# A gated mix of attention and a gated unit: a fixed table of seven PSUM banks, weights laid out by tiles, loads in order of use, maxima 20 steps ahead

## The chip, the cores and the metric

The kernel runs on one core of a Trainium2 chip. The metric is device time in microseconds (us); the kernel before takes 1745.21 us, the median of 3 runs (1744.91 to 1745.61). Smaller is better.

## What is computed

```python
def reference(x, wqkv, wo, w_gate, w_up, w_down, gate_w):     # x: 2048 x 512
    g = sigmoid((x * gate_w).sum(-1, keepdims=True))
    q, k, v = heads(x @ wqkv)                    # 32 heads of 16
    p = softmax(q @ k.T * 16 ** -0.5)            # per head, 2048 x 2048
    a = concat(p @ v) @ wo
    b = (sigmoid(x @ w_gate) * (x @ w_up)) @ w_down      # inner width 1792
    return g * a + (1 - g) * b
```

Everything is float32. Products of the projections are made of three products of a high and a low half each (`terms`, L126), so that the fast matmul form keeps the accuracy.

## The kernel before

The order of every engine's work is written out by hand: the program emits instructions in one stream, each engine keeps the order of emission, and waits come from the tiles that instructions share. PE is TensorE, ACT ScalarE, DVE VectorE, POOL GpSimd; SP only issues DMAs, in order.

**PSUM.** There are eight banks of 128 x 512: `st0..st2` (`banks`, L61), `dn` (L63), `sm0..sm3` (`maxb`, L65). `turns` (L54) hands out the banks of a list in rotation. A product may go into a bank only when the last reader of what stood there is done.

**Start (L222 to L346).** Twenty matmuls on zeros come first (`WARM`, L78). Then x is loaded in four chunks of 512 tokens (`load_x`, L179, one DMA for each 128 rows) and split into halves on ACT (high) and DVE (low) (`split_x`, L186). For each chunk, the first q tile and the first k tile are projected (12 matmuls each, L339 to L342) and put out to DRAM through ACT and DVE (`put_first`, L197); `load_pair` (L214) reads them back in the layout of a pair of heads, `QS` and `KS`. In chunk 3 the weights of v are split (L335 to L338). A weight tile is a block of 128 columns, loaded as 512 B rows (`raw_cols`, L105).

**Projection of v (L379 to L405).** Two token tiles at a time, each product cut into the lower and the upper 64 rows of the array (`Sum`, L135), so that two matmuls run side by side: one uses rows 0 to 63, the other rows 64 to 127. Between them run the first maxima: `first_max` (L322) makes steps 0 to 19 (`FIRST`) of the score maxima. At the end, `ahead` makes the first four score tiles. `turn` (L155) puts an empty instruction on POOL between two halves of a sum that write one bank: it waits for the first half, and the second half waits for it.

**The main loop (L534 to L565): 256 periods.** Softmax needs the maximum of each row of scores before the exponentials. So each period k has
- 4 + 4 score products of the pass for maxima, `m0` and `m1` (L254): rows 0 to 47 and 64 to 111 of the array for the two heads of a pair; DVE reduces each bank to one column (L256);
- 4 + 4 score tiles `t0` (this period's, lower rows) and `t1` (next period's, upper rows), L374; ACT takes the exponential of each (L376) into `p`;
- 6 + 6 half products of the side work `d1` (upper rows) and `d0` (lower rows), L146, into `dn`: projections of the other q and k tiles and of gate and up. Every second period a sum is finished, ACT copies it out (`leave`, L316), SP stores it;
- `values(k)` (L474): 8 products of v with p, in four column groups of the array at once (L482; the trace shows 16 instructions). They go into the next bank of the `st` list and are copied out by ACT (`part`, L487) and summed on POOL (L499).

The order of a period is the string `STEADY` (L526); the last 8 periods use `LAST`. The maxima run ahead of the exponentials: by 20 steps (a period is two steps) at first and, since one more product in each of the periods 0 to 3 (L546) moves them on, by 21 (`LEAD`) from there. When all 16 steps of half a pair are done, DVE reduces and transposes the maxima (L260, L262), POOL splits them, SP writes them to DRAM and reads them back into four rows of `QS` (`put_max`, L265); the score tiles of that half can only be made then.

The banks in the loop: `t0`, `t1` and `values` take `st0..st2` in rotation, nine uses a period; `m0`, `m1` take `sm0..sm3`. From the period in which the maxima are done, all seven are one list (`bank7`, L408).

**Behind the loop** follow the rest of the side work, the down projection and the output projection (L569 to L679), which the change leaves alone.

Of the kernel before, what the change touches and what calls it, by code (L numbers as in the profile page):

```python
# [34 lines left out]
FIRST = 20  # L35
LEAD = 21
WARM = 20
# [7 lines left out]
def gated_mix(ctx, tc, x, xT, wqkv, wo, w_gate, w_up, w_down, gate_w, out):  # L45
# [59 lines left out]
    def raw_cols(src, c0, name):  # L105
        return raw_weights(src[:, c0:c0 + P].rearrange("(k p) f -> p k f", p=P), [P, KT, P], name)
# [72 lines left out]
    def load_x(c):  # L179
        raw = mid(f"x{c}")  # L180
        cols = slice(c * 512, (c + 1) * 512)
        for k in range(KT):
            sp.dma_start(raw[:, k, :], xT[k * P:(k + 1) * P, cols])
        return raw

    def split_x(c, raw):  # L186
        cols = slice(c * 512, (c + 1) * 512)
        for k in range(KT):
            split(xh[:, k, cols], xl[:, k, cols], raw[:, k, :], act, dve)
# [35 lines left out]
    w_q = split_weights(raw_cols(wqkv, 0, "q0"), act, dve)  # L225
    xr = {0: load_x(0)}
# [3 lines left out]
    split_x(0, xr.pop(0))  # L230
    w_k = split_weights(raw_cols(wqkv, D, "k0"), act, dve)
# [33 lines left out]
    def put_max(half):  # L265
# [5 lines left out]
        def low():  # L271
# [3 lines left out]
            for b in range(2):  # L275
# [10 lines left out]
    def filling():  # L286
        jobs = [("qk", c) for c in range(1, D // P)] + [("gu", f) for f in range(NF)] + [("down", 0)]

        def raws(kind, n):
            if kind == "qk":  # L290
                return [raw_cols(wqkv, n * P, f"q{n}"), raw_cols(wqkv, D + n * P, f"k{n}")]
            if kind == "gu":
                return [raw_cols(w_gate, n * P, f"g{n}"), raw_cols(w_up, n * P, f"u{n}")]
# [25 lines left out]

    first = [(j, i) for j in [*range(0, 16, 2), *range(1, 16, 2), *range(16, FIRST)] for i in range(2)]  # L320

# [7 lines left out]
    for c in range(NC):  # L329
        if c + 1 < NC:  # L330
            split_x(c + 1, xr.pop(c + 1))
        if c == 0:
            wv_r = mid("wv_r")
            sp.dma_start(wv_r, wqkv[:, 2 * D:].rearrange("(k p) f -> p k f", p=P))
        if c == NC - 1:  # L335
# [3 lines left out]
        for w, dst in ((w_q, q_d), (w_k, k_d)):  # L339
            o = bank()  # L340
            product(o, unit(w, c))
            put_first(o, dst, c)  # L342
# [5 lines left out]
    bankv = turns(banks + [bankd()])  # L348
# [30 lines left out]
    bank = turns(banks[:2])  # L379
# [5 lines left out]
    for t in range(2, NS, 2):  # L385
        two = [Sum(bankv(), tokens(t + a)) for a in range(2)]
        for g in (LOW, UP):
            first_max()
            for m in range(3 * KT):
# [4 lines left out]
                if (0, 0) in mrow:  # L394
                    for step in put_max((0, 0)):
                        step()
                if t == NS - 2 and g == UP and m % 3 == 1:
# [10 lines left out]
    bank7 = turns(maxb + banks)  # L408
# [65 lines left out]
    def values(k):  # L474
# [10 lines left out]
        def put(e):  # L485
            if 2 * k + LEAD <= NSTEP:
# [16 lines left out]
    def mx(b):  # L503
        for j in range(FIRST, NSTEP):
# [11 lines left out]

    def emit(order, **parts):

        for kind in order.split():
            if kind == "turn":  # L520
                turn(run)
                work(1)
            else:
                next(parts[kind], None)

    STEADY = ("t0 m1 m0 d1 t0 d1 m0 d1 t0 d1 m0 d1 t0 d1 turn m0 t1 "  # L526
# [172 lines left out]
```

## Time and profile before

| | |
|---|---|
| median of 3 runs | 1745.21 us |
| the profiled execution | 1748.52 us, of which the span from the first to the last instruction is 1745.4 us |
| granted TensorE clock | 1.000 |
| busy: PE, DVE, ACT, POOL | 1737.6, 1426.0, 1318.7, 469.7 us |
| the main loop (products L482 of period 4 to those of period 244) | 118.58 to 1468.79 us |

A timeline row has the start in us from the span's start, the duration, the engine (PEld is the loading of weights on PE; SPq a DMA issue), line, operation, what is written and read, and how many instructions were merged; in brackets stands the idle time of the engine just before and what ended it. A row of the stretches has the stretch, its length, then busy time and instructions of each engine, the granted clock, the DMA share and GB/s. In the chain of waits each piece has start, duration, engine, tile and line.

### The profile page before, as it was taken

The numbers are of one execution on the slowest core, as the hardware profiler recorded it, in microseconds if no ns is written. First come the engines' busy times: TensorE is split into PE (matmuls) and PEld (weight loads), VectorE is DVE, ScalarE is ACT, GpSimd is POOL, SyncE is SP. The second block draws the span as 40 slices with busy tenths as digits, with TensorE's granted clock in tenths as the row PEclk, the third lists the DMA queues.
The fourth block names the chain that finished last, engine by engine and source line by source line (L and its number), as shares of the span: only waits on it lengthen the run. The fifth ranks groups of instructions, "written<-read, shape, count | busy, mean of one in ns | idle before, by whom it ended". The sixth has DMA issues, their size and how long they took to land.

```text
span 1745.4 us, 33221 instructions
## 1 busy us (share of the span) xinstructions
PE 1737.6 (100%) x12676; PEld 1041.8 (60%) x12676; DVE 1426.0 (82%) x2292; ACT 1318.7 (76%) x2554; POOL 469.7 (27%) x437
## 2 busy tenths in 40 slices
PE   9999999999999999999999999999999999999999
PEld 7755555555555555555555555555555555588887
DVE  5988888888988899989888888888888886357543
ACT  4188888888888888888888888888888888853321
POOL 1024343422231222222222222222222222352110
PEclk9999999999999999999999999999999999999999
DMA  8312424241313131414131313122121312367752
GB/s 248 80 32 68 92 68 92 68 105 44 81 52 76 41 87 51 86 51 87 38 75 39 68 39 62 51 55 53 50 51 49 63 45 80 105 228 247 258 193 73
DMA packets 99167, 149.74 MB, mean 86 GB/s; under 512 B 18816, under 2 KB 45440, under 8 KB 96128
## 3 DMA queue, kind: packets, MB, share of 16 engines
q1 hardware_dynamic: 99008, 147.63, 31.0%
q8 instruction: 99, 1.62, 0.4%
q14 instruction: 60, 0.49, 0.1%
HBM read 87.56 MB, written 60.03 MB: 85 GB/s over the span
## 4 chain that ended last, share of the span: by engine, by line
PE 96%; DVE 3%; DMA 1%; ACT 0%; issue 0%; POOL 0%; DVEq 0%; ACTq 0%; POOLq 0%
PE st L482 26%; PE st L374 20%; PE dn L146 18%; PE sm L254 16%; PE sm L662 7%; PE st L133 3%; DVE stat L256 2%; PE dn L662 2%; PE sm L571 1%; PE sm L482 1%; DMA k_d<-qe 1%; PE st L571 1%; PE st L146 1%; PE sm L374 0%; PE st L79 0%
## 5 line engine op out<-in xcount | busy, mean ns | idle before, releaser
L256 DVE TENSOR_REDUCE stat<-sm 128x1 f32<-128x512 f32 x2048 | 1250.1, 682 | 164.2 <-PE sm L254 138.3
L376 ACT ACTIVATE p<-st 128x512 f32<-128x512 f32 x2005 | 1012.4, 641 | 6.5 <-PE st L374 6.2
L374 PE MATMUL st<-qs,ks 64*128 64x512 f32 x2005 | 823.4, 423 | 0.0
L254 PE MATMUL sm<-ks,qs 48*128 48x512 f32 x2048 | 798.4, 417 | 0.4
L374 PEld LDWEIGHTS st<-qs,ks 64*128 64x128 f32 x2005 | 367.4, 184 | 327.5 <-ACT p L376 104.3
L499 POOL TENSOR_TENSOR sum<-sum,part 128x512 f32<-128x512 f32 x224 | 289.4, 1292 | 885.7 <-PE sm L254 674.9
L482 PE MATMUL st<-p,v 128*17 128x512 f32 x3984 | 476.1, 595 | 0.0
L254 PEld LDWEIGHTS sm<-ks,qs 48*128 48x128 f32 x2048 | 356.8, 185 | 61.1 <-DVE stat L256 16.4
L487 ACT ACTIVATE part<-st 128x512 f32<-128x512 f32 x215 | 128.6, 598 | 180.9 <-PE st L482 176.8
L482 PEld LDWEIGHTS st<-p,v 128*17 128x17 f32 x3984 | 92.3, 96 | 232.3 <-issue 156.0
L447 DVE TENSOR_TENSOR gul<-gul 128x1024 f32<-128x1024 f32 (+1 forms) x30 | 46.8, 1565 | 34.8 <-ACT gul L446 32.2
L316 ACT ACTIVATE gu<-dn 128x512 f32<-128x512 f32 x99 | 69.2, 699 | 0.0
L662 PE MATMUL sm<-wd_h,hl 128*128 128x512 f32 x208 | 67.0, 389 | 0.0
L95 ACT ACTIVATE hl<-gul 128x1024 fp32r<-128x1024 f32 (+1 forms) x30 | 29.8, 996 | 33.8 <-PE sm L662 22.0
L95 ACT ACTIVATE oh<-ot 128x1024 fp32r<-128x1024 f32 x8 | 8.5, 1062 | 59.9 <-DVE ot L620 59.9
L98 POOL TENSOR_TENSOR ol<-ot,oh 128x1024 fp32r<-128x1024 f32 x8 | 19.3, 2409 | 110.0 <-ACT oh L95 110.0
L98 DVE TENSOR_TENSOR hl<-gul,hl 128x1024 fp32r<-128x1024 f32 (+1 forms) x30 | 42.3, 1417 | 4.1 <-ACT hl L95 4.0
L662 PEld LDWEIGHTS sm<-wd_h,hl 128*128 128x128 f32 x208 | 39.0, 188 | 8.2
L487 ACT ACTIVATE sum<-st 128x512 f32<-128x512 f32 x31 | 18.5, 598 | 32.8 <-PE st L482 32.8
L662 PE MATMUL sm<-wd_l,hl 128*128 128x512 f32 x104 | 40.5, 389 | 0.0
L357 ACT ACTIVATE v<-st 128x512 f32<-128x512 f32 x12 | 6.9, 597 | 44.4 <-PE sm L254 25.2
L133 PE MATMUL st<-wohl,oh 128*128 128x512 f32 x128 | 39.4, 389 | 0.0
(454 smaller groups left out, 2821.4 us busy)
## 6 DMA issues: line engine op xcount, KB each, us to landing
gu_d<-gu SPq DMA_DIRECT2D x112, 256.0 KB
gul<-gu_d SPq DMA_DIRECT2D x56, 512.0 KB
qs<-q_d SPq DMA_DIRECT2D x90, 128.0 KB
ks<-k_d SPq DMA_DIRECT2D x90, 128.0 KB
pv_d<-sum SPq DMA_DIRECT2D x32, 256.0 KB
q_d<-qe SPq DMA_DIRECT2D x12, 512.0 KB
k_d<-qe SPq DMA_DIRECT2D x12, 512.0 KB
x<-in_xT_dram SPq DMA_DIRECT2D x16, 256.0 KB
```

Of the source, the lines that this page charges most:

```text
L98: lo.tensor_tensor(l, src, h.bitcast(F32), ALU.subtract)
L133: pe.matmul(o, a, b, start=(i == 0), stop=(i == len(ops) - 1))
L146: mm = pe.matmul(self.o, a[rows], b[rows], start=(self.n == 0), stop=(self.n == 2 * len(self.ops) - 1))
L254: pe.matmul(t, qs[r:r + KM, qt * P:(qt + 1) * P], ks[r:r + KM, g * 512:(g + 1) * 512], start=True, stop=True)
L256: dve.tensor_reduce(stat[half][:, b, qt % 8, g:g + 1], t, axis=AX.X, op=ALU.max)
L316: leave = lambda e, o: act.activation(e, o, AF.Copy)
L374: pe.matmul(o, ks[r:r + KR, (kt + a) * P:(kt + a + 1) * P], qs[r:r + KR, q0:q0 + 512], start=True, stop=True)
L376: act.activation(pt[:, 2 * a + c, :], o, AF.Exp, scale=DH ** -0.5)
L482: pe.matmul(o[32 * c:32 * c + VW, :], v[:, 2 * k % 16 + a, h * VW:(h + 1) * VW], pts[c // 2][:, 2 * a + c % 2, :], start=(a == 0), stop=(a ...
L487: act.activation(e, o, AF.Copy)
L499: pool.tensor_tensor(s, s, e, ALU.add)
L662: pe.matmul(down[t], a, b, start=(f == 0 and m == 0), stop=(f == NF - 2 and m == 5))
```

## The change

- **Banks.** In the loop each `t`, `m` names its bank in the order string, an index into `seven = sm0..sm3, st0..st2`: 0 to 3 are `sm`, 4 to 6 `st`. `values` always takes bank 0 (`SUMS`). The order of a period differs too: `m1` comes first, and in the first half the pieces of one row half come in twos (`d1 d1`).
- **Maxima.** `LEAD` is 20; `FIRST` and the extra maxima of periods 0 to 3 go. The maximum of half a pair is then complete at the end of a period, not three quarters through it. Its rows for the upper head are read back first.
- **Loads.** The host lays q, k, gate and up weights out by tiles, so that a partition's part of a tile is one run of 2 KB. At the start the order is q tile, x rows 0 and 1, k tile, x rows 2 and 3, and chunk 0 is projected in two parts: q and k with the first two row blocks, then q and k with the others. `WARM` is 10. The weights of v are split in chunk 2.
- **Last value tiles.** The v projection begins its rotation with `dn`, so that the last pair of tiles is in `st1` and `st2`, both copied out by ACT; `ahead` uses `dn` and `st0`, and its four tiles come three matmul pairs earlier. `put_max` of the first half is emitted a few matmuls later.

```diff
--- before.py
+++ after.py
@@ -32,9 +32,8 @@
 VROW = H * VW
 KM = 3 * DH
 KR = 64
-FIRST = 20
-LEAD = 21
-WARM = 20
+LEAD = 20
+WARM = 10
 NSTEP = NPAIR * 32
 NPER = NSTEP // 2
 TAIL = 8
@@ -42,7 +41,7 @@
 
 
 @with_exitstack
-def gated_mix(ctx, tc, x, xT, wqkv, wo, w_gate, w_up, w_down, gate_w, out):
+def gated_mix(ctx, tc, x, xT, wqk, wv, wo, w_gate, w_up, w_down, gate_w, out):
     nc = tc.nc
     pe, act, dve, pool, sp = nc.tensor, nc.scalar, nc.vector, nc.gpsimd, nc.sync
 
@@ -102,8 +101,8 @@
         sp.dma_start(raw, src)
         return raw, shape, name
 
-    def raw_cols(src, c0, name):
-        return raw_weights(src[:, c0:c0 + P].rearrange("(k p) f -> p k f", p=P), [P, KT, P], name)
+    def raw_cols(src, n, name):
+        return raw_weights(src[n], [P, KT, P], name)
 
     def split_weights(loaded, *engines):
         raw, shape, name = loaded
@@ -176,16 +175,16 @@
     gwb = xp.tile([P, D], F32, name="gwb")
 
 
-    def load_x(c):
-        raw = mid(f"x{c}")
+    def load_x(c, raw=None, ks=range(KT)):
+        raw = raw or mid(f"x{c}")
         cols = slice(c * 512, (c + 1) * 512)
-        for k in range(KT):
+        for k in ks:
             sp.dma_start(raw[:, k, :], xT[k * P:(k + 1) * P, cols])
         return raw
 
-    def split_x(c, raw):
+    def split_x(c, raw, ks=range(KT)):
         cols = slice(c * 512, (c + 1) * 512)
-        for k in range(KT):
+        for k in ks:
             split(xh[:, k, cols], xl[:, k, cols], raw[:, k, :], act, dve)
 
     def unit(w, c):
@@ -222,13 +221,17 @@
     act.activation(g1[:, :1], warm, AF.Exp)
     ones = v.rearrange("p t (h c) -> p t h c", c=VW)[:, :, :, DH]
     pool.memset(ones, 1.0)
-    w_q = split_weights(raw_cols(wqkv, 0, "q0"), act, dve)
-    xr = {0: load_x(0)}
+    raw_q = raw_cols(wqk, 0, "q0")
+    xr = {0: load_x(0, ks=(0, 1))}
+    raw_k = raw_cols(wqk, KT, "k0")
+    load_x(0, xr[0], (2, 3))
+    w_q = split_weights(raw_q, act, dve)
     for b in range(2):
         pool.memset(KS[b].bitcast(F32), -1.0)
         pool.memset(QS[b].bitcast(F32), 0.0)
-    split_x(0, xr.pop(0))
-    w_k = split_weights(raw_cols(wqkv, D, "k0"), act, dve)
+    split_x(0, xr[0], (0, 1))
+    w_k = split_weights(raw_k, act, dve)
+    split_x(0, xr.pop(0), (2, 3))
     xr.update((c, load_x(c)) for c in range(1, NC))
 
     stat = {}
@@ -272,7 +275,7 @@
             pool.tensor_tensor(hl[:, 1, :], mt, hl[:, 0, :].bitcast(F32), ALU.subtract)
             d = max_d[2 * p + i]
             sp.dma_start(d.rearrange("k r a j -> (k r) a j"), hl.bitcast(F32))
-            for b in range(2):
+            for b in (1, 0):
                 for a in range(2):
                     r = 64 * b + 3 * DH + a
                     sp.dma_start(QS[p % 2][r:r + 1, i * 1024:(i + 1) * 1024].rearrange(
@@ -288,9 +291,9 @@
 
         def raws(kind, n):
             if kind == "qk":
-                return [raw_cols(wqkv, n * P, f"q{n}"), raw_cols(wqkv, D + n * P, f"k{n}")]
+                return [raw_cols(wqk, n, f"q{n}"), raw_cols(wqk, KT + n, f"k{n}")]
             if kind == "gu":
-                return [raw_cols(w_gate, n * P, f"g{n}"), raw_cols(w_up, n * P, f"u{n}")]
+                return [raw_cols(w_gate, n, f"g{n}"), raw_cols(w_up, n, f"u{n}")]
             return [raw_weights(w_down[f * P:(f + 1) * P, :], [P, D], f"wd{f}") for f in range(2)]
 
         nxt = [split_weights(r) for r in raws(*jobs[0])]
@@ -317,7 +320,7 @@
     fill = filling()
 
 
-    first = [(j, i) for j in [*range(0, 16, 2), *range(1, 16, 2), *range(16, FIRST)] for i in range(2)]
+    first = [(j, i) for j in [*range(0, 16, 2), *range(1, 16, 2), *range(16, LEAD)] for i in range(2)]
 
     def first_max():
         if first:
@@ -331,21 +334,24 @@
             split_x(c + 1, xr.pop(c + 1))
         if c == 0:
             wv_r = mid("wv_r")
-            sp.dma_start(wv_r, wqkv[:, 2 * D:].rearrange("(k p) f -> p k f", p=P))
-        if c == NC - 1:
+            sp.dma_start(wv_r, wv.rearrange("(k p) f -> p k f", p=P))
+        if c == NC - 2:
             wv_h, wv_l = mid("wv_h", F32R), mid("wv_l", F32R)
             for k in range(KT):
                 split(wv_h[:, k, :], wv_l[:, k, :], wv_r[:, k, :], act, dve)
-        for w, dst in ((w_q, q_d), (w_k, k_d)):
-            o = bank()
-            product(o, unit(w, c))
-            put_first(o, dst, c)
+        two = [(bank(), list(terms(unit(w, c))), dst) for w, dst in ((w_q, q_d), (w_k, k_d))]
+        for part in ((0, 6), (6, 12)) if c == 0 else ((0, 12),):
+            for o, ops, dst in two:
+                for m in range(*part):
+                    pe.matmul(o, *ops[m], start=(m == 0), stop=(m == len(ops) - 1))
+                if part[1] == 12:
+                    put_first(o, dst, c)
         if c % 2:
             load_pair(0, slice((c - 1) * 512, (c + 1) * 512))
     sp.dma_start(gwb, gate_w.unsqueeze(0).to_broadcast([P, D]))
     next(fill)
     w_v = [(wv_h[:, k, :], wv_l[:, k, :]) for k in range(KT)]
-    bankv = turns(banks + [bankd()])
+    bankv = turns([bankd()] + banks)
 
     def tokens(t):
         return [((xh[:, k, t * P:(t + 1) * P], xl[:, k, t * P:(t + 1) * P]), w_v[k]) for k in range(KT)]
@@ -376,7 +382,7 @@
                 act.activation(pt[:, 2 * a + c, :], o, AF.Exp, scale=DH ** -0.5)
                 yield
 
-    bank = turns(banks[:2])
+    bank = turns([dn, banks[0]])
     ahead = st_part(0, 1)
     for t in range(2):
         o = bankv()
@@ -391,10 +397,10 @@
                 two[1].half(1 - g)
                 if m in (5, 11):
                     first_max()
-                if (0, 0) in mrow:
+                if (0, 0) in mrow and g == UP and m == 2:
                     for step in put_max((0, 0)):
                         step()
-                if t == NS - 2 and g == UP and m % 3 == 1:
+                if t == NS - 2 and (g, m) in ((LOW, 10), (UP, 1), (UP, 4), (UP, 7)):
                     next(ahead)
             if g == LOW:
                 turn(*two)
@@ -405,7 +411,8 @@
                 put_v(t + a, two[a].o, act)
 
 
-    bank7 = turns(maxb + banks)
+    seven = maxb + banks
+    bank7 = turns(seven)
     chunks = [(c, f) for c in range(NC) for f in range(0, NF, 2)]
 
     def hidden_load(c, f):
@@ -483,7 +490,7 @@
                           pts[c // 2][:, 2 * a + c % 2, :], start=(a == 0), stop=(a == 1))
 
         def put(e):
-            if 2 * k + LEAD <= NSTEP:
+            if 2 * k + LEAD < NSTEP:
                 act.activation(e, o, AF.Copy)
             else:
                 dve.tensor_copy(e, o)
@@ -501,7 +508,7 @@
                 sp.dma_start(pv_d[half[1], half[0]], s)
 
     def mx(b):
-        for j in range(FIRST, NSTEP):
+        for j in range(LEAD, NSTEP):
             one = sm_step(j)
             for i in range(2):
                 one(b, i)
@@ -514,26 +521,31 @@
             run.half(g)
             yield
 
+    spot = []
+
     def emit(order, **parts):
 
-        for kind in order.split():
-            if kind == "turn":
+        for word in order.split():
+            if word == "turn":
                 turn(run)
                 work(1)
             else:
+                kind, _, b = word.partition(":")
+                spot[:] = [seven[int(b)]] if b else []
                 next(parts[kind], None)
 
-    STEADY = ("t0 m1 m0 d1 t0 d1 m0 d1 t0 d1 m0 d1 t0 d1 turn m0 t1 "
-              "m1 d0 t1 d0 m1 d0 t1 d0 m1 d0 t1 d0")
+    STEADY = ("m1:3 t0:2 m0:4 d1 d1 t0:5 m0:6 d1 d1 t0:1 d1 m0:3 d1 t0:2 turn m0:0 t1:4 "
+              "m1:5 d0 d0 t1:1 t1:6 d0 m1:2 d0 m1:3 d0 t1:4 d0")
+    SUMS = 0
     LAST = "t0 d1 t0 d1 t0 d1 turn t0 t1 t1 d0 t1 d0 t1 d0"
 
     parts = {"m0": mx(0), "m1": mx(1), "d0": dense(LOW), "d1": dense(UP)}
-    bank = turns(banks)
-    for a, engine in enumerate((act, dve)):
-        put_v(NS - 2 + a, two[a].o, engine)
+    for a in range(2):
+        put_v(NS - 2 + a, two[a].o, act)
+    bank = bankm = lambda: spot[0]
     for k in range(NPER):
         n = 2 * k
-        if n + LEAD == NSTEP + 1:
+        if n + LEAD == NSTEP:
             bank = bank7
             leave = dve.tensor_copy
         if 128 <= n < 256 and n % 16 == 0:
@@ -543,8 +555,6 @@
         if n % 32 == 0 and n // 32 + 1 < NPAIR:
             load_pair(n // 32 + 1)
         parts["t0"], parts["t1"] = st_part(k, 0), st_part(k + 1, 1) if k + 1 < NPER else iter(())
-        if k < 4:
-            emit("m0" if k % 2 == 0 else "m1", **parts)
         emit(STEADY if k < NPER - TAIL else LAST, **parts)
         if k == NPER - 1:
             bankd = bank
@@ -557,6 +567,7 @@
         work(2)
         if k == NPER - 1:
             break
+        spot[:] = [seven[SUMS]]
         values(k)
         if n == NSTEP - 16:
             loaded.extend(hidden_load(*chunks[m]) for m in range(2))
@@ -680,10 +691,16 @@
 
 
 def kernel(A_x, A_wqkv, A_wo, B_x, B_w_gate, B_w_up, B_w_down, gate_w):
+    def by_tiles(w):
+
+        return np.asarray(w).reshape(KT, P, -1, P).transpose(2, 1, 0, 3)
+
+    wqkv = np.asarray(A_wqkv)
     host = {
         "x": np.asarray(A_x)[0],
         "xT": np.ascontiguousarray(np.asarray(A_x)[0].T),
-        "wqkv": A_wqkv, "wo": A_wo, "w_gate": B_w_gate, "w_up": B_w_up, "w_down": B_w_down, "gate_w": gate_w,
+        "wqk": by_tiles(wqkv[:, :2 * D]), "wv": wqkv[:, 2 * D:], "wo": A_wo,
+        "w_gate": by_tiles(B_w_gate), "w_up": by_tiles(B_w_up), "w_down": B_w_down, "gate_w": gate_w,
     }
     nc = bacc.Bacc("TRN2", target_bir_lowering=False, num_devices=1)
     arrays, args = {}, {}
```

## The prediction

> **What bounds the kernel now.** I read the page first, then one period of the loop in the timeline, then the chain of waits for the periods' spacing, then the start.
>
> ```profile
> span 1745.4 us, 33221 instructions
> PE 1737.6 (100%) x12676; PEld 1041.8 (60%) x12676; DVE 1426.0 (82%) x2292; ACT 1318.7 (76%) x2554; POOL 469.7 (27%) x437
> PE 96%; DVE 3%; DMA 1%; ACT 0%; issue 0%; POOL 0%; DVEq 0%; ACTq 0%; POOLq 0%
> ```
>
> PE looks like the bound: always busy, 96% of the chain. But a PE busy record also covers a matmul that is held up, so the loop must be read piece by piece.
>
> ```profile
> 722.35 0.18 PEld L374 LDWEIGHTS st<-qs,ks 64*128 64x128 f32 x1 [0.85 <-ACT gu L316]
> 722.55 0.60 ACT L487 ACTIVATE part<-st 128x512 f32<-128x512 f32 x1 [0.62 <-PE st L482]
> 722.70 0.39 PE L254 MATMUL sm<-ks,qs 48*128 48x512 f32 x1
> 722.70 0.19 PEld L374 LDWEIGHTS st<-qs,ks 64*128 64x128 f32 x1
> 722.92 4.88 DVE L256 TENSOR_REDUCE stat<-sm 128x1 f32<-128x512 f32 x8 [0.75 <-PE st L374]
> 722.93 0.40 PE L374 MATMUL st<-qs,ks 64*128 64x512 f32 x1
> 723.04 4.02 ACT L376 ACTIVATE p<-st 128x512 f32<-128x512 f32 x8
> 724.67 0.18 PEld L374 LDWEIGHTS st<-qs,ks 64*128 64x128 f32 x1
> 725.16 0.18 PEld L374 LDWEIGHTS st<-qs,ks 64*128 64x128 f32 x1
> 725.46 0.18 PEld L254 LDWEIGHTS sm<-ks,qs 48*128 48x128 f32 x1
> 725.49 0.47 PE L254 MATMUL sm<-ks,qs 48*128 48x512 f32 x1
> 725.65 0.18 PEld L374 LDWEIGHTS st<-qs,ks 64*128 64x128 f32 x1
> 725.80 0.39 PE L374 MATMUL st<-qs,ks 64*128 64x512 f32 x1
> 726.13 0.13 PEld L482 LDWEIGHTS st<-p,v 128*17 128x17 f32 x8 [0.30 <-ACT p L376]
> 727.98 0.18 PEld L374 LDWEIGHTS st<-qs,ks 64*128 64x128 f32 x1 [0.85 <-ACT p L376]
> ```
>
> This is one period, 722.35 to 727.98: 5.63 us. Call its start s. PE alone needs 14 pairs at 0.23 (722.70 to 722.93) and the values (726.13 to 727.98, 1.85), about 5.1. ACT makes eight exponentials in 4.02: one ends 0.60 after its start and the next starts 0.49 later. DVE makes eight maxima in 4.88: 0.69 alone (a row below), so (4.88 - 0.69) / 7 = 0.60 apart. Now the waits. The late `t1` loads stand at 724.67, 725.16, 725.65: 0.49 apart, ACT's pace, since each takes the bank that an exponential three before it gives back. The values take the next bank: exponential 6 ends at 723.04 + 5 x 0.49 + 0.60 = 726.09, and their load stands at 726.13. The last `m1` (725.46) waits for the maximum of the fourth, which ends at 722.92 + 3 x 0.60 + 0.69 = 725.41. From it PE can't go faster: its stream starts about 0.1 after the load, the last `t1` follows 0.23 later (725.80), the values 0.33 after that: 726.13 again. So two loops close at the same length: ACT's (part at s + 0.20, first exponential at s + 0.69, sixth done, values, next s) and DVE's (first maximum at s + 0.57, fourth done, last `m1`, last `t1`, values).
>
> **The change part by part.**
>
> *The bank table* frees the values from exponential 6. They take bank 0, read before by the fifth maximum (`m0:0`). I lay the new order on the same clock, from s: `m1:3` and `t0:2` start together as `t0` and `m1` did; part evicts bank 0 at s + 0.20, and the first exponential is behind it on ACT, s + 0.69, as now; the first maximum at s + 0.57. Exponential n ends at s + 1.29 + 0.49(n - 1), maximum n at s + 1.26 + 0.60(n - 1). What waits: `m0:3` for maximum 1 (s + 1.26), the second `t0:2` for exponential 1 (1.29), `t1:4` for maximum 2 (1.86), `t1:1` for exponential 3 (2.27), `t1:6` for maximum 3 (2.46), `m1:2` for exponential 4 (2.76), the last `m1:3` for maximum 4 (3.06), the last `t1:4` for exponential 5 (3.25), the values for maximum 5 (3.66). All tiles are ready before ACT or DVE come to them, so both keep their pace. The end: last `m1` loads at 3.11, streams at 3.22, last `t1` at 3.45, values at s + 3.78. That is 726.13 - 722.35 = 3.78: the chain through maximum 4 is untouched, and the order at the end (`d0 m1 d0 t1 d0`) is the same. Only ACT's loop is relieved, 5.63 against 5.62 for DVE's. I take 0.005 us a period; the ends are a gain of 0.01 and, as the rows agree no better, 0.03 either way.
>
> ```profile
> 94.44 1.84 PE st L482 x16
> 118.58 1.86 PE st L482 x16
> 1468.79 1.86 PE st L482 x16
> 109.09 5.47 DVE L256 TENSOR_REDUCE stat<-sm 128x1 f32<-128x512 f32 x9 [0.70 <-PE st L374]
> 115.31 4.88 DVE L256 TENSOR_REDUCE stat<-sm 128x1 f32<-128x512 f32 x8 [0.74 <-PE st L374]
> 1474.60 0.21 DVE L262 STREAM_TRANSPOSE mt<-mpad 128x32 f32<-128x32 f32 x1 [0.47 <-DVE mpad L260]
> ```
>
> From the values of period 4 to those of period 244 there are 240 periods, (1468.79 - 118.58) / 240 = 5.626 each. The table: -1.2, ends -7 and +7.
>
> *LEAD 20.* Periods 0 to 3 have nine maxima now, not eight, and take (118.58 - 94.44) / 4 = 6.04. At 5.63 they give back 1.6. The four maxima go to period 245, where ACT's loop hides them. The half-pair's closing (reduce and transpose, 0.4 to 0.9 with the idle time shown) moves behind the eighth maximum, s + 5.46, while the next first maximum is due at 5.63 + 0.57 = 6.20: nothing, at worst 0.2 at 31 ends. The rows reach `QS` later: transposed at about s + 6.2, two POOL instructions (0.6), a store, then reads 2.4 after it (rows below), two for the upper head, 0.7 each, 2.4 to land: s + 12.9 at the most. The first `t1` of that half is due at 2 x 5.63 + 1.9 = 13.2. Covered, by little; the upper head's rows coming first is what covers it.
>
> ```profile
> 0.92 7.02 PE L79 MATMUL st<-warm 128*128 128x512 f32 x20 [0.92 <-DVE warm L76]
> 3.00:4.00 1.00, 1.00 (x3) 0.79 (x3) 0.00 (x0) 0.16 (x1) 1.00 (x2) 1.00 0.85 283
> 6.00:7.00 1.00, 1.00 (x6) 0.86 (x6) 0.00 (x0) 0.63 (x1) 1.00 (x2) 1.00 0.71 174
> 8.10 1.31 ACT L95 ACTIVATE xh<-x 128x512 fp32r<-128x512 f32 x2 [1.11 <-DMA x<-in_xT_dram]
> 13.50 0.39 PE L133 MATMUL st<-xh,q0h 128*128 128x512 f32 x1
> 15.90 10.99 DMA k_d<-qe
> 24.57 0.60 ACT L204 ACTIVATE qe<-st 128x512 fp32r<-128x512 f32 x1 [2.75 <-PE st L133]
> 27.48 2.18 ACT L95 ACTIVATE wv_h<-wv_r 128x512 fp32r<-128x512 f32 x4
> 31.37 0.50 PE L133 MATMUL st<-wv_h,xh 128*128 128x512 f32 x1 [1.39 <-DVE qe L205]
> 37.04 0.50 PE L254 MATMUL sm<-ks,qs 48*128 48x512 f32 x2
> 30.44 2.90 SPq L220 DMA_DIRECT2D ks<-k_d x6
> 78.63 0.34 SPq L274 DMA_DIRECT2D max_d<-mhl x1
> 81.04 2.92 SPq L278 DMA_DIRECT2D qs<-max_d x4
> ```
>
> *The start.* Chunk 1 begins at 13.50, behind zeros until 7.9 and then x. With ten zeros PE is free at about 5, but x row 2 arrives at 8.10 and the k tile is now ahead of it, say 8.8; high and low split (0.63, 0.69), then six products of q and six of k at 0.23 each put chunk 1 at about 13.1: -0.4. Then 12 matmuls x 0.23 six times, to 29.4. Now the v projection waits until 31.37, for `st0`: the v split (27.48) sits on ACT and DVE ahead of chunk 3's evictions. In the new order the split is done in chunk 2, where ACT idles 2.75 ahead of 24.57, and the first value tile goes to `dn`. So it starts at 29.4 instead of 31.37, and the first maximum at 35.1 instead of 37.04; the last `ks` load is issued at about 33 and lands 2.4 later (store to read above), 35.3. I take -1.8. Ends: 0 if x or the v weights come late enough, -2.1. DVE then paces the projection, so the shift carries to its end.
>
> On the weights' layout: while the q tile's 512 B rows were moved, 283 GB/s (3 to 4 us). The Trainium skill ("DMA: Bandwidth & Descriptors", Specifications) puts the least transfer for full rate at 512 B, so by it longer runs gain nothing; no run here shows longer ones for this tile. I take nothing, with up to 0.4 more in the ends.
>
> ```profile
> 81.92 6.07 DVE L256 TENSOR_REDUCE stat<-sm 128x1 f32<-128x512 f32 x10 [0.32 <-PE sm L254]
> 90.81 0.46 PE L146 MATMUL dn<-xh,q1h 64*128 64x512 f32 x1 [0.69 <-DVE v L359]
> ```
>
> *Last value tiles and the first `put_max`.* The 0.32 on DVE goes, since POOL's pieces of `put_max` no longer stand ahead of the empty instruction that PE waits for: -0.3. The 0.69 ahead of period 0 goes with DVE's copy, but bank 5 and 6 now wait for ACT's two copies (0.49 + 0.60): I take -0.2, ends -0.7 and +0.4. *The change of lists* in period 246: its first `t0` takes bank 0, which part holds until s + 0.80, and it is first in PE's queue: +0.4, ends 0 and +0.85.
>
> Sum: -1.2 - 1.6 - 1.8 - 0.3 - 0.2 + 0.4 = -4.7. The profiled execution took 1748.52 with a span of 1745.4; the runs' median is 1745.21, 0.2% less, and the sum is taken from it: 1740.5. Its own ends are 1738 and 1743.7. About 0.2%, 3.5 us, can be told from no change.
>
> **The rivals.**
>
> *The start gives nothing* (1742.3). Speaks for it: the zeros run at half the pace first, three or four a us at 3 to 4, six at 6 to 7, so the clock came up at about 6, though its column says 1.00; ten zeros end before that, and then PE waits for x. If twelve or more products run at half pace, 12 x 0.23 = 2.7 are lost, all of the gain. Against it: the holes are under 1 us. The Trainium skill ("TensorE: Matmul & The Clock Gate", Part 1) says the clock rises after about 3.4 us of activity and falls after an idle window of 3.4 us, the window running free; by that it would stay up here; no run shows it yet.
>
> *The values come early* (1722): if the last `m1` is not held by maximum 4, the values start at maximum 5, s + 3.70, period 5.55: 240 x 0.08 = 19 more. Against it stands the row at 725.46.
>
> *DVE becomes the bound* (1752, slower). The values now wait for the fifth maximum, with a slack of 0.07 or 0.08: from where it ends after s + 3.73, each 0.1 costs 24 us. Two of the five running alone (0.69 instead of 0.60) would do it: 0.18 - 0.08 = 0.10. I price half of that, +12. For it: the small slack. Against: eight maxima in 4.88 in every period.
>
> *Row halves in twos don't overlap* (about 1950). The same page (Part 3, What overlaps) says weights load under a running matmul only where the row group differs. The trace disagrees: at 722.70 the load of a `t0` runs under the `m0` of the same rows. Were it so, seven more such neighbours a period would add 7 x 0.18 = 1.3, from PE's own 3.06 for the last pair to 4.35, 0.9 past today's 3.45: 240 x 0.9 = 216 more.
>
> **How the numbers follow.** Forecast 0.52, start 0.20, early values 0.12, DVE 0.11, twos 0.05. The forecast's ends straddle 1741.7: 0.37 faster, 0.15 same. Faster 0.37 + 0.12 + 0.02 of the start case = 0.51; same 0.15 + 0.18 + 0.01 = 0.34; slower 0.15. The range takes in the first two cases and the nearer half of the next two, 1730 to 1750; the likeliest case's own is 1738 to 1743.7.
>
> **What would show it.** Right: values spaced 5.62 from period 0 on; the load of the last `m1` still 0.05 behind the fourth maximum's end; first maximum product at about 35.1; no 0.69 at the loop's start. Wrong: a spacing off 5.62 by over 0.02; half-pair ends with a longer period (rows of maxima late); products at half pace after 6 us.

## The result, and the profile after

The changed kernel takes 1733.06 us, the median of 4 runs (1732.68 to 1733.95), beside 1745.41 for the kernel before (1744.91 to 1746.88, 4 runs): 12.35 us less, a ratio of 0.9929 (0.9911 to 0.9946). Its profiled execution took 1733.32 us with a span of 1731.5.

The page of the changed kernel (span; busy time of each engine; shares of the chain of waits):

```profile
span 1731.5 us, 33713 instructions
PE 1724.6 (100%) x12666; PEld 1066.3 (62%) x12666; DVE 1426.1 (82%) x2291; ACT 1319.3 (76%) x2555; POOL 471.0 (27%) x437
PE 97%; DVE 2%; DMA 0%; ACT 0%; issue 0%; SPq 0%; DVEq 0%
```

DVE and ACT have the same work: 1426.0 and 1318.7 before, 1426.1 and 1319.3 after. PE's busy time fell with the span, but as the prediction says it also covers matmuls that are held up. So the page doesn't show where 12 us went: the time is in waits. The chain of waits gives the spacing (start, duration, tile and line of the products of the values, periods 0, 4, 244, 245, 246):

```profile
91.11 1.84 PE sm L489 x16
113.43 1.85 PE sm L489 x16
1454.42 1.84 PE sm L489 x16
1459.99 0.90 PE sm L489 x5
1466.01 1.84 PE sm L489 x16
```

Periods 0 to 3 take (113.43 - 91.11) / 4 = 5.58 (6.04 before), periods 4 to 243 (1454.42 - 113.43) / 240 = 5.587 (5.626 before): 240 x 0.039 = 9.3 us of the 12.35. Period 245 takes 6.02. It took 5.17 before, by the loads of the values in the timeline of before:

```profile
1474.36 0.13 PEld L482 LDWEIGHTS st<-p,v 128*17 128x17 f32 x8 [0.30 <-ACT p L376]
1479.53 0.13 PEld L482 LDWEIGHTS sm<-p,v 128*17 128x17 f32 x8 [0.36 <-ACT p L376]
```

That is the change of lists, +0.85. So the gain lies where the prediction took almost nothing. One period of the changed kernel in the timeline, from the first load of scores to the next:

```profile
724.14 0.18 PEld L257 LDWEIGHTS sm<-ks,qs 48*128 48x128 f32 x1 [0.85 <-DVE stat L259]
724.14 0.18 PEld L380 LDWEIGHTS sm<-qs,ks 64*128 64x128 f32 x1
724.33 0.60 ACT L494 ACTIVATE part<-sm 128x512 f32<-128x512 f32 x1 [0.63 <-issue]
724.67 0.69 DVE L259 TENSOR_REDUCE stat<-sm 128x1 f32<-128x512 f32 x1 [0.71 <-PE sm L380]
724.82 0.59 ACT L382 ACTIVATE p<-sm 128x512 f32<-128x512 f32 x1
726.48 1.28 DVE L259 TENSOR_REDUCE stat<-sm 128x1 f32<-128x512 f32 x2
727.20 0.66 ACT L382 ACTIVATE p<-sm 128x512 f32<-128x512 f32 x1
727.21 0.18 PEld L257 LDWEIGHTS sm<-ks,qs 48*128 48x128 f32 x1
727.56 0.39 PE L380 MATMUL st<-qs,ks 64*128 64x512 f32 x1
727.88 0.13 PEld L489 LDWEIGHTS sm<-p,v 128*17 128x17 f32 x8 [0.27 <-DVE stat L259]
729.72 0.18 PEld L257 LDWEIGHTS sm<-ks,qs 48*128 48x128 f32 x1 [0.85 <-DVE stat L259]
```

With s = 724.14: the first maximum starts at s + 0.53, where it was 0.57. The fourth (the first of the two merged at 726.48, 0.68 each) ends at 726.48 + 0.68 = 727.16; the last `m1` loads 0.05 later, at 727.21, as before; then the last `t1` (727.56) and the values (s + 3.74, before 3.78). The chain through maximum 4 is still the one that ends last. It begins 0.035 earlier (medians of 232 periods: 0.570 before, 0.535 after). The sixth exponential ends at 727.20 + 0.66 = 727.86 and no longer holds the values.

The start of the changed kernel (timeline, PE alone: zeros, products of the first q and k tiles, chunk 1, first maximum product):

```profile
0.92 4.63 PE L78 MATMUL st<-warm 128*128 128x512 f32 x10 [0.92 <-DVE warm L75]
5.34 0.47 PE L346 MATMUL st<-xh,q0h 128*128 128x512 f32 x1
5.65 0.41 PE L346 MATMUL st<-xl,q0h 128*128 128x512 f32 x1
5.90 0.40 PE L346 MATMUL st<-xh,q0l 128*128 128x512 f32 x1
7.51 0.49 PE L346 MATMUL st<-xh,q0h 128*128 128x512 f32 x1 [1.22 <-ACT xh L94]
8.82 0.40 PE L346 MATMUL st<-xh,k0h 128*128 128x512 f32 x1
9.05 0.40 PE L346 MATMUL st<-xl,k0h 128*128 128x512 f32 x1
12.95 0.39 PE L346 MATMUL st<-xh,q0h 128*128 128x512 f32 x1
34.80 0.51 PE L257 MATMUL sm<-ks,qs 48*128 48x512 f32 x2
```

The first maximum product stands at 34.80, 2.24 ahead of the 37.04 before. The experiments show that more than half of this difference belongs to the one execution of before that was profiled.

### The profile page after: what moved, and what is told of

The parts are those of the page before. It is cut to its first block, busy times and chain, and to the rows that moved or that the text cites. A ratio compares the mean times of both kernels' runs of the same rounds, so it can differ in the third digit from the quotient of the medians.

```text
span 1731.5 us, 33713 instructions
## 1 busy us (share of the span) xinstructions
PE 1724.6 (100%) x12666; PEld 1066.3 (62%) x12666; DVE 1426.1 (82%) x2291; ACT 1319.3 (76%) x2555; POOL 471.0 (27%) x437
## 4 chain that ended last, share of the span: by engine, by line
PE 97%; DVE 2%; DMA 0%; ACT 0%; issue 0%; SPq 0%; DVEq 0%
PE dn L145 29%; PE sm L489 27%; PE sm L257 12%; PE sm L673 7%; PE st L380 7%; PE sm L380 5%; PE st L132 3%; PE st L257 2%; DVE stat L259 2%; PE dn L673 2%; PE st L346 1%; PE sm L582 1%; PE st L582 1%; PE st L145 1%; PE st L489 0%; DMA x<-in_xT_dram 0%
## 5 line engine op out<-in xcount | busy, mean ns | idle before, releaser
L259 DVE TENSOR_REDUCE stat<-sm 128x1 f32<-128x512 f32 x1310 | 848.9, 684 | 154.8 <-PE sm L380 138.0
L382 ACT ACTIVATE p<-st 128x512 f32<-128x512 f32 x1019 | 612.8, 654 | 2.3 <-PE st L380 2.3
L382 ACT ACTIVATE p<-sm 128x512 f32<-128x512 f32 x1027 | 604.8, 630 | 2.4 <-PE sm L380 1.8
L257 PE MATMUL sm<-ks,qs 48*128 48x512 f32 x1310 | 521.0, 436 | 0.2
L489 PE MATMUL sm<-p,v 128*17 128x512 f32 x4048 | 483.8, 595 | 0.0
L259 DVE TENSOR_REDUCE stat<-st 128x1 f32<-128x512 f32 x738 | 482.6, 682 | 0.1
L380 PE MATMUL sm<-qs,ks 64*128 64x512 f32 x1027 | 426.9, 421 | 0.8 <-ACT part L494 0.8
L380 PE MATMUL st<-qs,ks 64*128 64x512 f32 x1019 | 423.3, 419 | 0.0
L257 PE MATMUL st<-ks,qs 48*128 48x512 f32 x738 | 291.4, 395 | 0.0
L380 PEld LDWEIGHTS sm<-qs,ks 64*128 64x128 f32 x1027 | 188.7, 185 | 12.7 <-issue 4.3
```

The lines of the kernel that those rows point to most:

```text
L257: pe.matmul(t, qs[r:r + KM, qt * P:(qt + 1) * P], ks[r:r + KM, g * 512:(g + 1) * 512], start=True, stop=True)
L259: dve.tensor_reduce(stat[half][:, b, qt % 8, g:g + 1], t, axis=AX.X, op=ALU.max)
L380: pe.matmul(o, ks[r:r + KR, (kt + a) * P:(kt + a + 1) * P], qs[r:r + KR, q0:q0 + 512], start=True, stop=True)
L382: act.activation(pt[:, 2 * a + c, :], o, AF.Exp, scale=DH ** -0.5)
L489: pe.matmul(o[32 * c:32 * c + VW, :], v[:, 2 * k % 16 + a, h * VW:(h + 1) * VW], pts[c // 2][:, 2 * a + c % 2, :], start=(a == 0), stop=(a ...
```

## The experiments

**The theory.** Before, two loops closed at nearly the same length, ACT's through the sixth exponential and DVE's through the fourth maximum. The table opens only ACT's. The new order puts `m1` ahead of `t0` in the first pair, and that alone makes the first maximum 0.035 earlier and opens only DVE's. Either alone gains little; both give 0.04 a period. The rivals: the whole gain comes from the twos, from the table, or from the start. Each run stood beside the kernel before on the same chip (1745.49, 1745.78 or 1745.64 us); "spacing" is that of the values of periods 4 and 244, as above.

| run | us | ratio (95%) | spacing |
|---|---|---|---|
| `t0` first in the changed kernel | 1740.72 | 0.9972 (0.9961 to 0.9982) | 5.619 |
| `m1` first in the kernel before | 1744.45 | 0.9994 (0.9985 to 1.0004) | 5.620 |
| values in a bank that ACT reads | 1742.82 | 0.9984 (0.9975 to 0.9994) | 5.628 |
| row halves alternating | 1734.89 | 0.9941 (0.9926 to 0.9955) | 5.595 |
| new start, old loop | 1744.91 | 0.9995 (0.9986 to 1.0005) | 5.630 |
| before with 20 steps | 1745.65 | 0.9999 (0.9990 to 1.0009) | 5.634 |
| changed kernel, 20 zeros | 1733.70 | 0.9932 (0.9917 to 0.9947) | 5.587 |
| changed kernel, last list turned | 1732.83 | 0.9925 (0.9910 to 0.9940) | 5.587 |
| before, once more | 1745.52 | 0.9997 (0.9987 to 1.0008) | 5.626 |
| old start, new loop | 1733.53 | 0.9930 (0.9916 to 0.9945) | 5.581 |
| before, 20 steps, upper head first | 1743.39 | 0.9987 (0.9978 to 0.9996) | 5.626 |
| changed kernel, lower head first | 1735.17 | 0.9940 (0.9927 to 0.9953) | 5.597 |

### `t0` first in the changed kernel

```diff
-    STEADY = ("m1:3 t0:2 m0:4 d1 d1 t0:5 ...
+    STEADY = ("t0:2 m1:3 m0:4 d1 d1 t0:5 ...
```

> The changed kernel with the first two words of the period exchanged: t0:2 ahead of m1:3. Theory (two loops were tied; the table cut ACT's, and putting m1 first cut DVE's, since the first maximum starts 0.535 us after s instead of 0.570): the first maximum goes back to about 0.57, the values to 3.775 after s, the spacing from 5.587 to about 5.62, the time up by 8 us to about 1741. Rival A (the table alone made the gain): spacing 5.59, time 1733. Rival B (the pairs of like row halves made it): spacing 5.59, time 1733.

1740.72 us: the swap of two names in the string costs 7.7 of the 12.35 us (240 x 0.032, from the spacing). Timeline, first load and first maximum of a period:

```profile
727.52 0.18 PEld L380 LDWEIGHTS sm<-qs,ks 64*128 64x128 f32 x1 [0.85 <-DVE stat L259]
728.09 0.69 DVE L259 TENSOR_REDUCE stat<-sm 128x1 f32<-128x512 f32 x1 [0.74 <-PE sm L257]
```

The first maximum is back at 728.09 - 727.52 = 0.57. The two products still load and stream in the same hundredth of a us; only their order in the queue differs.

### `m1` first in the kernel before

```diff
-    STEADY = ("t0 m1 m0 d1 t0 d1 ...
+    STEADY = ("m1 t0 m0 d1 t0 d1 ...
```

> The kernel before with m1 ahead of t0 in the period and nothing else. Theory: the first maximum starts about 0.035 us earlier, but the values still wait for the sixth exponential (3.785 after s), so the spacing stays at 5.626 and the time at 1745 (within 2 us). If m1 first were enough by itself: spacing 5.59, time 1736 to 1737.

1744.45 us, not to be told from no change. Timeline of one period:

```profile
730.48 0.18 PEld L254 LDWEIGHTS sm<-ks,qs 48*128 48x128 f32 x1 [0.85 <-DVE stat L256]
731.02 3.68 DVE L256 TENSOR_REDUCE stat<-sm 128x1 f32<-128x512 f32 x6 [0.70 <-PE st L374]
734.26 0.13 PEld L482 LDWEIGHTS st<-p,v 128*17 128x17 f32 x8 [0.30 <-ACT p L376]
```

The maximum is early (0.54), yet the values load at 734.26 - 730.48 = 3.78 as ever, because they still wait for the sixth exponential. One loop is opened and the other holds.

This run holds a second experiment that nobody planned. In every eighth period (30 of the 240) ACT copies the values into `sum` and not into `part`, and this copy starts 0.14 behind s, not 0.20 (timeline: first load of scores, copy and next load of the values, in one such period and in the one after it):

```profile
814.82 0.18 PEld L254 LDWEIGHTS sm<-ks,qs 48*128 48x128 f32 x1 [0.85 <-DVE stat L256]
814.96 0.60 ACT L487 ACTIVATE sum<-st 128x512 f32<-128x512 f32 x1 [1.05 <-PE st L482]
818.56 0.13 PEld L482 LDWEIGHTS st<-p,v 128*17 128x17 f32 x8 [0.32 <-ACT p L376]
820.40 0.18 PEld L254 LDWEIGHTS sm<-ks,qs 48*128 48x128 f32 x1 [0.85 <-DVE stat L256]
820.60 0.60 ACT L487 ACTIVATE part<-st 128x512 f32<-128x512 f32 x1 [0.63 <-PE st L482]
824.18 0.13 PEld L482 LDWEIGHTS st<-p,v 128*17 128x17 f32 x8 [0.30 <-ACT p L376]
```

So ACT's loop is 0.06 shorter in these periods, with no edit of the program. The median period is then 5.578 with `m1` first (this run) and 5.617 with `t0` first (the kernel before); in all other periods it is 5.626 and 5.627. Both openings together give 0.049, ACT's alone 0.010 and the early maximum alone 0.001. The spacing of 5.620 in the list of runs is the mean of the two kinds.

### Values in a bank that ACT reads

```diff
-    SUMS = 0
+    SUMS = 1
```

> The changed kernel with the values in bank 1, which the sixth exponential gives back, instead of bank 0. Theory: the values start 0.05 us behind the sixth exponential's end again, 3.775 to 3.785 after s, spacing about 5.62, time up by 8 us to about 1741, though m1 is first. Rival A (m1 first alone made the gain): spacing 5.59, time 1733.

1742.82 us, somewhat above what was expected. Bank 1 is last read by the sixth exponential, and the trace names it (timeline, sixth exponential and load of the values in one period):

```profile
731.85 0.65 ACT L382 ACTIVATE p<-sm 128x512 f32<-128x512 f32 x1
732.55 0.13 PEld L489 LDWEIGHTS sm<-p,v 128*17 128x17 f32 x8 [0.30 <-ACT p L382]
```

It ends at 732.50, the values load 0.05 later. With ACT's loop closed again, the early maximum is worth nothing, as in the run before. (Seven periods of this run are 0.2 to 0.3 longer, 1.8 us in all; they are treated at the end.) These three runs settle the loop: both openings are needed.

### Row halves alternating

```diff
-    STEADY = ("m1:3 t0:2 m0:4 d1 d1 t0:5 m0:6 d1 d1 t0:1 d1 m0:3 d1 t0:2 turn m0:0 t1:4 "
-              "m1:5 d0 d0 t1:1 t1:6 d0 m1:2 d0 m1:3 d0 t1:4 d0")
+    STEADY = ("m1:3 t0:2 m0:4 d1 t0:5 d1 m0:6 d1 t0:1 d1 m0:3 d1 t0:2 d1 turn m0:0 t1:4 "
+              "m1:5 d0 t1:1 d0 t1:6 d0 m1:2 d0 m1:3 d0 t1:4 d0")
```

> The changed kernel with upper and lower row halves alternating all through the period (m1 t0 m0 d1 t0 d1 m0 d1 ...), the banks and their order as changed. Theory: the late products wait for the same maxima and exponentials, so spacing 5.587 within 0.005 and time 1733 within 2 us. Rival B (like halves in twos made the gain): spacing 5.62, time 1741. If twos cost something: below 1732.

1734.89 us. The twos don't bring the gain, and they cost nothing: without them the kernel is slower by some 1.8 us, 0.008 a period.

### New start, old loop

The kernel before with the start, loads, layout and last value tiles of the changed one, but the old loop and 21 steps. It also has the upper head's rows first.

```diff
-WARM = 20
+WARM = 10
...
-    w_q = split_weights(raw_cols(wqkv, 0, "q0"), act, dve)
-    xr = {0: load_x(0)}
+    raw_q = raw_cols(wqk, 0, "q0")
+    xr = {0: load_x(0, ks=(0, 1))}
+    raw_k = raw_cols(wqk, KT, "k0")
...
-    for a, engine in enumerate((act, dve)):
-        put_v(NS - 2 + a, two[a].o, engine)
+    for a in range(2):
+        put_v(NS - 2 + a, two[a].o, act)
```

> The kernel before with the new start, loads and value tiles alone (weights by tiles, order of loads, ten zeros, split of v's weights in chunk 2, dn first), LEAD 21 and the old banks and order of the loop. From the two traces this part gave 3.3 us up to the first values (94.37 to 91.04): time about 1742, spacing 5.626, first maximum product at about 34.9. If part of the 3.3 came with the loop's first period instead: 1743.

1744.91 us: a miss. The expectation, 1742 or 1743, was read from the two profiled starts (3.3 us up to the first values), and 0.9 came. Four periods of the loop are 0.28 to 0.29 longer than the rest, 1.1 us, which takes back part of the gain.

### Before, once more

No edit; the question is how far one profiled start stands for the others.

> The kernel before, unchanged, profiled once more. Theory: the start in the profile of before was late by some 2 us, because one store of the first k tile took 10.99 us and the eviction of chunk 2 stood behind it; a second execution shows the first maximum product at 34.5 to 35.3 us, values of period 0 at about 92.0, and a span of 1742 to 1744. Rival (the late start belongs to the kernel): 37.0 and 94.4 again. Either way the median is 1745.5.

The median is 1745.52 again. In the first profile of before, the eviction of a k tile in the start (timeline, ACT) was held by a DMA, and in the second not; the third line is the first maximum product of the second profile:

```profile
26.99 0.60 ACT L204 ACTIVATE qe<-st 128x512 fp32r<-128x512 f32 x1 [1.82 <-DMA k_d<-qe]
```

```profile
24.94 0.60 ACT L204 ACTIVATE qe<-st 128x512 fp32r<-128x512 f32 x1 [1.05 <-PE st L133]
35.71 0.50 PE L254 MATMUL sm<-ks,qs 48*128 48x512 f32 x2
```

It is the store of 10.99 us that the prediction quotes. The expectation (34.5 to 35.3) was a little too early, 37.0 is refuted. Over all traces at hand, the first maximum product stands at 34.7 to 37.0 in six executions with the old start (mean 35.6) and at 34.0 to 34.8 in eight with the new (mean 34.4). So the new start gains about 1.2 up to there, not 2.24, and 0.9 (35.3 to 34.4) without the first profile of before. The starts differ in more than the store. Twenty zeros took 7.02 us in the first profile, and in this one (timeline, PE):

```profile
0.92 7.62 PE L79 MATMUL st<-warm 128*128 128x512 f32 x20 [0.92 <-DVE warm L76]
```

The profiled execution of before (1748.52) lay 3.3 above its median. Its start is 1.7 later than the mean of the other five. Another 1.3 or so lies outside the span: 1748.52 - 1745.4 = 3.1, where the other profiled executions have 1.7 to 2.1.

### 20 zeros in the changed kernel

```diff
-WARM = 10
+WARM = 20
```

> The changed kernel with twenty zeros again instead of ten. Theory: the second block of x is not there before 6.8 us, so the zeros that end at 7.9 hold up three products that would have run before it: 0.2 to 0.4 us later at the first maximum product, time 1733 to 1734. If the zeros were what held the start: the first maximum product at 36 or later, time 1735.

1733.70 us: the ten zeros are worth 0.6 at most, which isn't told from nothing. The cause that was expected doesn't show either: the first maximum product of this profile stands at 34.34, not later than the 34.80 of the changed kernel but 0.46 earlier, and both lie in the scatter of the starts.

### 20 steps in the kernel before

```diff
-LEAD = 21
+LEAD = 20
...
-        if k < 4:
-            emit("m0" if k % 2 == 0 else "m1", **parts)
```

> The kernel before with the maxima 20 steps ahead all through and nothing else. Theory: periods 0 to 3 take 5.63 instead of 6.04, the rest 5.626: 1.6 to 1.8 us less, time about 1743.6. If the later rows of maxima were late for their first t1 somewhere, a longer period at half-pair ends, up to 31 of them, and 1745 or more.

1745.65 us: a miss. Periods 0 to 3 give back their 1.7 (5.62 each), but two later periods take 6.73 and 6.36. In the first of them (timeline, a score product):

```profile
310.88 0.47 PE L374 MATMUL st<-qs,ks 64*128 64x512 f32 x1 [0.95 <-DMA qs<-max_d]
```

The product waits for the rows of the maxima, which arrive too late: 1.1 + 0.7 us lost, and 0.3 in a third period, somewhat more than the 1.7 gained. What is late is the store of the maxima ahead of the reads (chain of waits):

```profile
303.20 3.40 DMA max_d<-mhl
```

By the semaphore times of this trace, 24 of the 32 such stores are complete 1.4 to 1.5 us after their issue; in the others the last of 16 signals comes later, up to this 3.4. The kernel before has such stores too (up to 3.5), and with 21 steps its longest period from 4 to 243 is 5.70. This is the wait that the prediction feared, and this kernel lacks the edit that was to cover it. The next two runs test that edit by itself.

### 20 steps and the upper head first, in the kernel before

```diff
-            for b in range(2):
+            for b in (1, 0):
                 for a in range(2):
                     r = 64 * b + 3 * DH + a
```

with the edit of the run before.

> The kernel before with 20 steps ahead and the upper head's rows read back first. Theory: in the run with 20 steps alone, the gain of 1.7 in periods 0 to 3 was eaten by two periods of 6.73 and 6.36 us, in which a score product waited 0.95 us for the rows of maxima; with the upper head first no period is over 6, and the time is 1743.7. Rival (the order of the rows changes nothing, the long periods come from the stores ahead of them): 1745.6.

1743.39 us, 2.26 less than the run without the edit: no period from 4 to 243 is longer than 5.64, though one of its stores takes 3.3 us again. The order of the reads is what covers a late store.

### The lower head first, in the changed kernel

The same edit the other way round.

> The changed kernel with the rows of the lower head read back first, as before. Theory: some closings of a half pair come late again, with periods above 6 us, more than two of them since the period is shorter: 1735 to 1737. Rival (the order of the rows is worth nothing here): 1733.1 with no period above 5.85.

1735.17 us, and periods 102, 198 and 214 take 6.03, 6.13 and 6.73; period 174 takes 5.84. In the longest (timeline):

```profile
1292.98 0.18 PEld L380 LDWEIGHTS st<-qs,ks 64*128 64x128 f32 x1 [1.23 <-DVE stat L259]
```

The releaser named, DVE's maximum, had long been done. The trace's semaphore times name the late one: the last of the four reads of rows lands at 1292.88, 0.10 ahead of this load. In the run with 20 steps it lands at 310.74, 0.11 ahead of the load that waited there. Two kernels, both directions: 2 us for the order of four small reads.

### Old start, new loop

The kernel before with 20 steps, the upper head first, the table and the order of the changed kernel, and nothing else.

```diff
+    STEADY = ("m1:3 t0:2 m0:4 d1 d1 t0:5 ...
+    SUMS = 0
...
+    bank = bankm = lambda: spot[0]
...
+        spot[:] = [seven[SUMS]]
         values(k)
```

> Start and loads of before, but the table, the new order, 20 steps and the upper head's rows first. Theory: the loop gives nearly all: spacing 5.587 from period 4 on, 5.59 in periods 0 to 3, 6.02 at the change of lists; with the start worth 0.9 (the start-only run), 1733.1 + 0.9 = 1734.0. Rival (the start is worth the 3.3 that the two profiles differ by): 1736.4.

1733.53 us, 12.1 below before. The chain of waits, values of periods 4 and 244:

```profile
115.11 1.84 PE sm L483 x16
1454.61 1.84 PE sm L483 x16
```

(1454.61 - 115.11) / 240 = 5.581. The loop, with the 20 steps and the upper head first, gives the result; all edits of the start together move it by a few tenths, which can't be told from nothing.

### The last list turned

At the change of lists the seven banks are dealt from `sm1` on, so that the first score tile no longer takes bank 0.

```diff
-    bank7 = turns(seven)
+    bank7 = turns(seven[1:] + seven[:1])
```

> The changed kernel with the list of seven banks for the last periods turned by one, so that the first t0 after the maxima takes bank 1 and not bank 0, which the part of the values before it still holds. Theory: the distance from the values of period 245 to those of period 246 goes from 6.02 back to 5.17, time 0.8 less, about 1732.2; everything else unchanged.

1732.83 us. The chain of waits, values of periods 244, 245, 246:

```profile
1453.61 1.85 PE sm L489 x16
1459.20 1.84 PE sm L489 x16
1464.38 1.84 PE sm L489 x16
```

Period 245 takes 1464.38 - 1459.20 = 5.18 again, so the 0.85 was the wait for bank 0. It is the fastest version measured, though 0.2 to 0.9 us (beside the changed kernel, and beside the run with 20 zeros on the same chip) is less than can be told from no change.

## Why the prediction was right in its direction and too small

| step | predicted | measured |
|---|---|---|
| table and order, periods 4 to 243 | -1.2 | -10.7 with the old start (5.626 to 5.581), -9.3 in the changed kernel |
| 20 steps | -1.6 | -1.7 in periods 0 to 3 |
| start, up to the first maximum | -1.8 | -0.9 to -1.2 between means of profiles |
| `v` projection | -0.3 | not to be told from the scatter |
| first period | -0.2 | -0.45, of which 20 steps have a part |
| change of lists | +0.4 | +0.85 |

*The table* is the term that was mis-sized, and its own ends (7 either way) didn't hold it. Nor did the sum's own ends of 1738 to 1743.7, which are narrower than the table's own: with -7 in place of -1.2 the sum gives 1734.7. That the wider 1730 to 1750 holds the 1733.06 is luck: its lower end comes from the rival of the early values, and that rival fell. The step that failed is "`m1:3` and `t0:2` start together as `t0` and `m1` did", with the first maximum at s + 0.57. They do start together. But of two products side by side the one issued first releases its reader 0.035 earlier (0.535 against 0.570, in both pairs of kernels that differ in this), and `m1` is now that one. The prediction saw that two loops were tied at 5.62 and 5.63, that the table opened one, and that the chain through maximum 4 was left; it costed the order inside the pair at nothing. The rest of that chain held to a hundredth: load 0.05 behind maximum 4, then the last `t1`, then the values 0.33 later. With the table alone (`t0` first) the spacing is 5.619, and the median period 5.613: 0.007 to 0.013 a period, somewhat more than the 0.005 that was taken.

*20 steps.* The size was right, and so was the remark that the upper head's rows coming first is the cover. Its price without that, which the prediction didn't give, is about 2 us.

*The start.* "I take -1.8" was read from the `v` projection at 31.37, which was said to wait for evictions behind the split of v. What made them so late was a store of 10.99 us, in an execution 0.2% above the median; the prediction noted that 0.2% and still read the stage from it. What it said of the new start held: 29.4 for the `v` projection and 35.1 for the first maximum product, with 29.27 and 34.80 in the profile of the changed kernel. The start that it was set against did not. In time the start gives less than the 1.2: 0.9 alone (with the last value tiles), 0.2 on top of the new loop, both within what can't be told from nothing. A part goes into the loop: kernels with the new start have some periods that are 0.2 to 0.3 longer (seven in the changed kernel, 1.6 us in all). The new loop with the old start has four that are 0.08 to 0.09 longer, 0.35 us in all, and the kernel before none above that. The first period, from the last product of the `v` projection to the first values, goes from 4.54 to 4.08. The new start alone gives 4.12 and the 20 steps alone 4.27, so the two share the 0.45; with 20 steps given, both value tiles through ACT are worth the 0.2 that was taken. A gain in the `v` projection couldn't be separated from the scatter of starts. The layout by tiles was not tried alone.

*The change of lists* hit its upper end: the first `t0` waits for bank 0, and nothing covers it.

*The rivals.* "The start gives nothing" nearly held in its result, and not by its mechanism, which was twelve or more products at half the pace. The first products of the changed kernel begin 0.31 and 0.25 apart (5.34 to 5.90), and behind the hole of 1.22 us on PE they run at 0.23 from 8.82 on: the clock didn't come down. The Trainium skill ("TensorE: Matmul & The Clock Gate", Part 1) has it fall only after an idle window of about 3.4 us. The hole of 1.22 us agrees with that. "The values come early" fell, since the last `m1` is still held by maximum 4; but a shorter loop did come, from the other end of the chain: 0.045 a period, where that rival had 0.08. "DVE becomes the bound" fell: the values load 0.12 behind the end of the fifth maximum. "Twos don't overlap" fell by 1734.89 against 1733.06.

*Order inside a pair.* Why the first of two products releases its reader earlier isn't settled; the trace shows when readers start, not when a product is announced. The second product of the pair begins 0.003 us behind the first, so the 0.035 isn't a later start. The Trainium skill ("TensorE: Matmul & The Clock Gate", Part 3, the cost: per-tile semaphore tail) says that the signals of products that end together go out one after another, 26 ns each. The 0.035 us measured is of that kind and somewhat more. No run here changed the number of signals.

## What to carry to other kernels

Where two loops are tied, opening one shows next to nothing (0.010 and 0.001 us a period here, against 0.049 for both) and the second edit gets all the credit: cost each alone and both together, and look at what begins each loop as closely as at what ends it. Of two operations that run side by side, issue first the one whose reader starts the longest chain. And when the profiled execution is slower than the median, find the stage that holds the excess before costing an edit in that stage.

## What the runs showed that was not expected

*The order of two names in a string.* The order of two products that load and stream together moves a reader by 0.035 us, and here 240 periods by 7.7 us.

*Periods that are long, and the profile doesn't show why.* In the changed kernel periods 40, 80, 90, 139, 149, 208 and 218 take 5.78 to 5.85 instead of 5.58. In the one that begins at 593.67, ACT is late by 0.28 (timeline):

```profile
595.98 0.60 ACT L494 ACTIVATE part<-sm 128x512 f32<-128x512 f32 x1 [1.34 <-issue]
```

It waits for nothing named. So it is in periods 149 and 218; in the other four the copy is in time and the first exponential starts 0.24 to 0.28 late. In each of the seven, and of the eighteen such periods of three other kernels, a transfer of instructions begins between 3.0 and 8.1 us after the period's values. There are 64 such transfers in the changed kernel, most of them beside no long period. That fetching is the cause isn't shown, and the order of time speaks against these transfers as what ACT waited for: in the period above the transfer begins at 596.63, 0.65 behind the late copy, and in periods 80 and 208 it begins 7.9 and 8.0 us behind the values, when the long period is over. The cause stays open, and so does which edit of the start brings these periods.
